# Another hand-written order for all 923 operations of a convolution and feed-forward kernel

## The chip, the cores and the metric

The kernel runs on one core of a Trainium2 chip. The core has a matrix engine (TensorE, PE in the profile), a vector engine (VectorE, DVE), a scalar engine (ScalarE, ACT), GpSimd (POOL), and SyncE (SP), whose work here is to issue DMAs. The engines run side by side; each takes its own instructions strictly in order, and waits on semaphores for what other engines and DMAs deliver. The metric is the time of one execution in microseconds (us), lower is better; a version's time is the median of its runs.

## The reference

One block of a network on a sequence of 2048 rows with 640 channels. A layer norm, a gated long convolution and a residual come first, then a second layer norm and a gated feed-forward layer (width 1728) with its own residual:

```python
def _A_ref(q, k, v, shift_k, ssm_k, ssm_D):          # q is layernorm(x)
    k_shift = sum over 4 taps t of k_pad[:, t:t+S, :] * shift_k[:, 3-t]
    kv = k_shift * v
    y = irfft(rfft(pad(kv)) * rfft(pad(ssm_k)))[:S]    # causal convolution over the sequence, per channel
    y = y + kv * ssm_D
    return q * y
def _B_ref(x, w_gate, w_up, w_down):
    return (silu(x @ w_gate) * (x @ w_up)) @ w_down
x  = A_q
h  = x + _A_ref(_layernorm(x), A_k, A_v, A_shift_k, A_ssm_k, A_ssm_D)
h2 = h + _B_ref(_layernorm(h), B_w_gate, B_w_up, B_w_down)
```

Inputs and output are bf16.

## The kernel before, in words

**Blocks.** The sequence is cut into four blocks (0 to 3) of 512 rows, each spread as 128 partitions by 4 rows (called r below). The convolution is done with transforms of length 1024 as matrix products: the filter block g (`load_g`, L289) is turned (`g_turned`) and transformed into a spectrum G; the block of k is turned and run through the four taps on PE (`kv_of`, L490), multiplied by v on DVE (L513 for block 0, L515 for the others), and transformed into a spectrum X (`transform`, PE L329, evicted from PSUM by ACT at L319 or by DVE at L322). `mac` (L524 to L594) adds up the products X[i]·H[j-i] on DVE, partly by accumulating DMAs which POOL issues (L243). `inverse` (L651) prepares sums and differences on DVE (L662 to L687), goes back through PE (L698), and ACT and DVE (L707, L709) apply the first layer norm, the gate and the residual. `turn_h` normalises the rows (L722 on ACT or L724 on DVE) and turns them, by DMA for blocks 1 and 2 (L404), by PE for blocks 0 and 3. `ffn` does gate and up products (PE L769), silu on ACT (L783), the product with `up` (either L785 on ACT followed by L787 on DVE, or L786 on DVE alone), and the down product (PE L845).

**Loads.** k comes by plain loads for block 0 and by transposing DMAs for the rest; g of blocks 1 to 3 is turned by ACT (L419) and transposing DMAs (L404); x, v and the weights come by plain loads (L301, L296, L737, L747).

**What sets the order.** The functions don't issue anything. Each calls `plan.add` and leaves an operation with a number, counted in the order of the calls. `Plan.run` then goes through the tuple `ORDER` (L47 to L89), which names every operation once, and issues them in that order. Since every engine has one queue, `ORDER` is the order of work on each engine and on SP's and POOL's DMA queues. Where an entry is negative, operation `~i` (one less than the number without the sign) goes to its other engine: a copy or product of ACT goes to DVE, a load of SP goes to POOL, an addition of DVE becomes an accumulating DMA of POOL. `ORDER` also decides which storage a tile gets: `Plan.run` hands out the 4 PSUM slots, the rows and the 22 units of the arena at the first use and takes them back after the last, so that another order makes other tiles share a unit, and with it other waits.

Operations spoken of below:

| number | what it is |
|---|---|
| 16, 17; 26; 27 | loads of k, v and x of block 0 |
| 12; 13, 14 | load of g of block 0; the two halves of the forward matrix WF |
| 186; 192; 191 | loads of g, x and v of block 1 |
| 194 to 197; 187 to 190 | the transposing DMAs of g and of k of block 1 |
| 97 | eviction of half a plane (128x320) of X of block 0 |
| 531 | normalised row (r = 1) of block 2 for the feed-forward part |
| 532, 534, 536, 538 | the four transposing DMAs of those rows of block 2 |
| 566 | the up product of one pair of chunks (128x1024) in block 1's feed-forward part; its L787 is 567 |
| 585, 803 | the up product of the odd chunk (128x512) in block 1's and block 2's feed-forward part; their L787 are 586 and 804 |
| 621 | load of v of block 3, which DVE's L515 reads |
| 714 | the first layer norm's power of block 3, on POOL |
| 715 to 720; 724 | DVE's preparation of the last inverse; its first product on PE |
| 829 | five chunks of a down product of block 2 |

A load's engine is chosen here:

```python
def load(nbytes, fn, w, r=()):
    return plan.add("sp", nbytes, lambda: fn(nc.sync), r, w, ("pq", nbytes, lambda: fn(nc.gpsimd)))
```

## Time and profile before

| | before |
|---|---|
| runs, us | 250.96, 251.34, 253.92; median 251.34 |
| span of the profiled execution, us | 251.4 |
| busy: PE, DVE, ACT, POOL | 94%, 79%, 69%, 21% |
| granted TensorE clock | 1.000 |
| DMA: bytes, share of the 16 engines | 33.66 MB; SP's queue 32.1%, POOL's 25.9% |

The profiled execution's own time is its span, 251.4 us, which is the median of the runs to 0.1 us; nothing lies around it that has to be added. The profile lists for each engine when it was busy and what ended each of its waits. PE's ends are modelled, because its matmuls are pipelined, so that a busy PE is not a PE at its peak; for PE the spacing of the starts in a run of equal matmuls is the better measure.

### The profile page before, as it was taken

What the parts mean: (1) busy time and instruction counts of PE and PEld (TensorE: products, weight loads), DVE (VectorE), ACT (ScalarE), POOL (GpSimd) and SP (SyncE); (2) the same over time, 40 slices, a digit from 0 to 9 for tenths busy, and PEclk for the clock granted to TensorE, in tenths of its full rate; (3) what the DMA queues carried; (4) which work ended last, traced back from release to release, by engine and by line L of the source; (5) the groups of instructions that cost most, each with busy time, mean ns of one, the idle gap of its engine ahead of it and who ended that gap; (6) DMA issues with size and microseconds to landing.
All of it is one profiled execution on the core that took longest, in us unless ns stands there. A gap on an engine that the chain in (4) does not pass through costs nothing.

```text
span 251.4 us, 5138 instructions
## 1 busy us (share of the span) xinstructions
PE 237.3 (94%) x2113; PEld 153.0 (61%) x2125; DVE 197.7 (79%) x249; ACT 173.9 (69%) x300; POOL 54.0 (21%) x54
## 2 busy tenths in 40 slices
PE   3869997999999999999999999999999999999994
PEld 3447675788777677444465676454456785465662
DVE  2379999999999999999999989999999542131222
ACT  2449998999999976975988789983542865325100
POOL 0002003231540313220270404263612110000030
PEclk9999999999999999999999999999999999999999
DMA  5995699774998654685345468889592200000052
GB/s 156 376 212 163 127 324 352 231 197 92 165 246 292 202 81 81 105 154 133 79 66 146 86 99 194 148 146 163 98 224 29 26 0 3 0 0 3 0 78 78
DMA packets 37283, 33.66 MB, mean 134 GB/s; under 512 B 22470, under 2 KB 32076, under 8 KB 37260
## 3 DMA queue, kind: packets, MB, share of 16 engines
q1 hardware_dynamic: 31884, 21.38, 32.1%
q0 software_dynamic: 5376, 11.96, 25.9%
q8 instruction: 16, 0.26, 0.4%
q14 instruction: 7, 0.06, 0.1%
HBM read 16.29 MB, written 4.59 MB: 83 GB/s over the span
## 4 chain that ended last, share of the span: by engine, by line
PE 56%; ACT 17%; DMA 10%; DVE 9%; issue 4%; SPq 3%; DVEq 0%; ACTq 0%; POOLq 0%
PE ps L769 24%; PE ps L845 22%; ACT arena L319 7%; DMA arena<-in_A_ssm_k_dram 7%; PE ps L698 5%; DMA arena<-arena 3%; ACT sg L785 2%; PE ps L490 2%; SPq L404 2%; ACT junk L606 1%; PE ps L329 1%; PE ps L833 1%; DVE arena L674 1%; DVE arena L663 1%; DVE arena L662 1%
## 5 line engine op out<-in xcount | busy, mean ns | idle before, releaser
L769 PE MATMUL ps<-arena,wgu 128*128 128x512 bf16 (+1 forms) x668 | 116.7, 328 | 1.4 <-ACT sg L809 0.5
L769 PEld LDWEIGHTS <-wgu 128*128 128x128 bf16 x680 | 66.2, 98 | 45.3 <-issue 1.4
L845 PE MATMUL ps<-wd,tT 128*128 128x320 bf16 x416 | 59.1, 299 | 0.0
L845 PEld LDWEIGHTS <-tT 128*128 128x128 bf16 x416 | 39.8, 98 | 17.2 <-issue 1.8
L542 DVE TENSOR_TENSOR arena<-arena 128x2560 bf16<-128x2560 bf16 x30 | 44.1, 1484 | 0.2
L783 ACT ACTIVATE sg<-ps 128x1024 bf16<-128x1024 f32 (+1 forms) x28 | 26.9, 968 | 20.3 <-PE ps L769 19.7
L329 PE MATMUL ps<-arena,WF 128*128 128x320 bf16 x176 | 29.8, 299 | 1.2 <-ACT arena L319 0.9
L785 ACT CAST sg<-ps 128x1024 bf16<-128x1024 f32 (+1 forms) x23 | 23.0, 998 | 6.9 <-PE ps L769 3.1
L319 ACT CAST arena<-ps 128x320 bf16<-128x320 f32 (+1 forms) x48 | 25.2, 583 | 1.9 <-DVE arena L545 1.1
L610 POOL TENSOR_TENSOR sm<-sm,neghalf 128x4 f32<-128x4 f32 (+1 forms) x10 | 16.6, 1659 | 43.4 <-DVE sm L646 43.1
L787 DVE TENSOR_TENSOR tT<-sg,sg 128x1024 bf16<-128x1024 bf16 (+1 forms) x23 | 15.5, 673 | 11.5 <-ACT sg L785 11.5
L243 POOL DMA_DIRECT2D arena<-arena x11 | 13.3, 1211 | 47.4 <-DVE arena L542 11.2
L329 PEld LDWEIGHTS <-WF 128*128 128x128 bf16 x176 | 17.1, 98 | 10.0 <-issue 2.3
L606 ACT ACTIVATE junk<-arena 128x640 bf16<-128x640 bf16 x28 | 20.8, 744 | 1.3 <-DVE arena L709 1.3
L545 DVE TENSOR_TENSOR arena<-arena 128x2560 bf16<-128x2560 bf16 x14 | 20.7, 1487 | 0.2
L319 ACT ACTIVATE arena<-ps 128x640 bf16<-128x640 f32 (+1 forms) x32 | 20.2, 655 | 0.3
L698 PE MATMUL ps<-arena,WI 128*128 128x320 bf16 x96 | 15.7, 299 | 0.9 <-issue 0.6
L850 ACT ACTIVATE row<-ps,sm 128x640 bf16<-128x640 f32 x12 | 9.5, 791 | 8.2 <-PE ps L845 8.0
L709 DVE SCALAR_TENSOR_TENSOR arena<-arena,sm,ps 128x640 bf16<-128x640 bf16 x16 | 13.6, 876 | 1.8 <-ACT ps L707 1.8
L852 POOL DMA_DIRECT2D out_dram<-row x12 | 11.7, 1153 | 14.1 <-ACT row L850 14.1
L707 ACT ACTIVATE ps<-ps,sm 128x640 f32<-128x640 f32 x16 | 12.1, 770 | 3.7 <-PE ps L698 3.5
L698 PEld LDWEIGHTS <-WI 128*128 128x128 bf16 x96 | 9.0, 97 | 5.6 <-issue 1.3
(91 smaller groups left out, 240.8 us busy)
## 6 DMA issues: line engine op xcount, KB each, us to landing
arena<-arena POOLq DMA_DIRECT2D x11, 640.0 KB, 6.1
arena<-in_A_q_dram SPq DMA_DIRECT2D x4, 640.0 KB, 5.1
out_dram<-row POOLq DMA_DIRECT2D x13, 160.0 KB, 4.2
arena<-in_A_ssm_k_dram SPq DMA_DIRECT2D x3, 640.0 KB, 9.4
arena<-in_A_v_dram SPq DMA_DIRECT2D x3, 640.0 KB, 6.3
wd<-in_B_w_down_dram SPq DMA_DIRECT2D x2, 800.0 KB, 7.3
out_dram<-arena POOLq DMA_DIRECT2D x2, 640.0 KB, 5.8
wgu<-in_B_w_gate_dram SPq DMA_DIRECT2D x1, 800.0 KB, 6.5
```

The lines of the kernel that those rows point to most:

```text
L319: (lambda: nc.scalar.activation(dst(), src(), ACT.Copy, scale=2.0)) if twice else (lambda: nc.scalar.copy(dst(), src())),
L329: nc.tensor.matmul(ap(ps)[:, h, 0:NH], w, ap(src)[:, r, h * NH:(h + 1) * NH], start=(first and i == 0), stop=(last and i == len(rs) - 1), ...
L542: dve(1402, lambda: v.tensor_mul(to(), X.part(xs), H.part(hs)), [X.at(xs), H.at(hs)], [at])
L545: added(1402 * n - 69 * (n - 1), lambda: v.tensor_add(to(), to(), b()), to, b, [what], at, n)
L606: act(725, lambda r=r: nc.scalar.activation(waste(), ap(x)[:, r, :], ACT.Square, scale=D ** -0.5, accum_out=sm(s, MSQ, (r,))), [(x, r)], [ ...
L610: nc.gpsimd.tensor_tensor(sm(s, RSTD, rs), sm(s, VAR, rs), ap(neghalf)[:, 0:len(rs)], op=ALU.pow)
L698: nc.tensor.matmul(ap(ps)[:, w, 0:NH], m, src[:, w * NH:(w + 1) * NH], start=(i == 0), stop=(i == len(terms) - 1))
L769: nc.tensor.matmul(split(ap(ps), n)[:, i, :], w(k), ap(hT)[:, k, lo:lo + n], start=(k == 0), stop=(k == KT - 1))
L783: act(905 if wide_ else 490, lambda: nc.scalar.activation(of(sg), of(*gate), ACT.Silu), [(gate[0], gate[1] + i) for i in range(m)] + (psu ...
L785: op = plan.add("act", 905 if wide_ else 490, lambda: nc.scalar.copy(of(co), of(*up)), psu + [sg], [co] + tt, ("dve", 1135 if wide_ else 6 ...
L787: op.rest = dve(602 if wide_ else 336, lambda: nc.vector.tensor_mul(to(), of(sg), of(co)), [sg, co], tt)
L845: nc.tensor.matmul(ap(ps[hf])[:, hf, 0:NH], ap(tT)[:, c * BLK + at:c * BLK + at + P], ap(wd)[:, c, hf * NH:(hf + 1) * NH], start=False, st ...
```

## The change

The code is the same but for the tuple `ORDER`: all 923 operations are still there, each once, and nothing is computed otherwise. The order of nearly all of them is another one on every engine and queue. The new tuple takes 42 lines in place of 43, so that every line behind it has a number one less. What else follows from it:

- **Engines.** Among SP's and POOL's DMAs, one goes elsewhere: 621, the load of block 3's v, is issued by SP, right behind the turns 532, 534, 538, 536 of block 2, and no longer by POOL. (The loads 616 of block 3's g, and the stores 308, 757 and 902 stay with POOL.) Of the copies and products, 97, 531, 566, 748 and 894 go from ACT to DVE in the new order, and 585, 803, 745 and 876 from DVE to ACT; of block 0's four k evictions two instead of three are DVE's (21, 23 for 19, 21, 25), of its four g evictions three as before (35 for 37).
- **Start.** SP's loads were k, shift taps, k, g1, v0, WF, skip, g0, WF, x0, WI, WI; they are k, taps, k, v0, g1, g0, WF, WF, skip, x0, one weight load of 640 KB, WI, WI.
- **Block 1.** SP's queue was: a turn of g1, x1's load (192), two turns of g1, then k1's turns with the last of g1's; it is: the eight turns (195, 194, 190, 196, 189, 197, 187, 188) and x1's load behind them. The turned g1 takes arena unit 4, which g0's raw tile held before it; in the old order it had unit 16.
- **Last inverse.** DVE's order was 715, 716, 717, 718, 719, 720; it is 715, 716, 718, 717, 720, 719. On PE, 829 stood ahead of 724 and stands behind it.
- **POOL's queue.** The stores 600, 615, 605, 610 of block 1 stand between the accumulating DMAs of block 3's `mac` instead of behind them, 757 stands ahead of them, and 714 behind them.

The diff, cut to the lines with those parts:

```diff
--- before.py
+++ after.py
 ORDER = (
-    0, 1, 2, 3, 16, 18, -20, 5, 4, 8, 17, 186, 9, 20, 22, 7, 10, 11, -22, 24, -26, 23, 26, 75, 76, 13, 15, 12, 6,
-    77, 78, 79, 193, 80, 81, 82, 34, 35, 14, 38, -40, 36, -38, 92, 32, 27, 93, 96, 97, 40, -42, 88, 89, 30, 94,
...
-    67, 68, 125, 115, 126, 116, 111, 112, 194, 198, 192, 199, 117, 69, 70, 195, 59, 60, 71, 72, 196, 200, 201, 63,
-    64, 61, 62, 73, 74, 127, 212, 65, 130, 66, 128, 202, 213, 207, 129, 134, 208, 131, 187, 203, 189, 197, 214,
-    215, 216, 190, 209, 210, 204, 133, 205, 270, 188, 221, 224, 225, 223, 175, 132, 138, 122, 211, 206, 217, 143,
...
-    631, 510, 514, 521, 522, 570, 573, 574, 644, 526, 622, -646, 595, 611, 617, 511, 515, 516, 512, 517, 518, 687,
-    525, 601, 612, 524, 527, 523, 528, 710, 682, 529, 530, 535, -534, 534, 531, 537, 532, 594, 596, 713, 646, 538,
...
-    598, 536, 806, 599, 805, 808, 650, 766, 765, 807, 809, 810, 811, 693, 709, 652, 654, 653, -622, 655, 695,
...
-    796, 798, 799, 812, 814, 815, 816, 705, 715, 716, 717, 718, 719, 600, 720, 605, 610, 817, 813, -758, 818, 819,
-    820, 821, 822, 823, 829, 724, 737, 723, 735, 738, 740, 736, 824, 830, 741, 739, 742, 743, 721, 725, 831, 832,
...
+    17, 8, 16, 1, 2, 0, 26, 186, 5, 3, 24, 7, 22, 4, -24, 9, 18, 10, 25, 11, 19, 20, -22, 75, 76, 77, 78, 79, 12,
+    80, 81, 82, 13, 83, 6, 40, -42, 38, 14, -40, 30, 193, 36, 37, 34, -36, 92, 93, 101, 102, 32, 96, -98, 94, 15,
+    95, 88, 89, 103, 104, 98, 84, 42, 85, 27, 120, 119, 118, 121, 90, 91, 99, 43, 44, 86, 87, 47, 48, 105, 106, 45,
+    46, 55, 56, 49, 174, 50, 51, 52, 107, 108, 29, 33, 57, 113, 58, 114, 53, 54, 100, 109, 124, 28, 110, 123, 126,
+    67, 68, 115, 116, 195, 111, 125, 194, 190, 112, 117, 69, 70, 198, 199, 31, 71, 72, 127, 196, 59, 60, 200, 201,
+    63, 189, 64, 73, 197, 61, 74, 130, 62, 212, 213, 187, 122, 65, 66, 128, 207, 208, 188, 202, 203, 192, 129, 214,
...
+    570, 521, 595, 611, 522, 644, 525, 573, 574, 526, 512, 517, 518, 511, 515, 706, 601, 602, 603, 612, -646, 516,
+    -758, 594, 606, 524, 527, 681, 523, 707, 528, 713, 682, 709, 687, 613, 596, 607, 529, 530, 614, 535, -532, 532,
+    537, -534, 534, 712, 604, 708, 538, 597, 598, 599, 647, 651, 649, 646, 608, 805, 536, 678, 648, 685, 677, 609,
+    650, 693, 680, 806, 810, 809, 765, 652, 807, 653, 600, 808, 811, 615, 766, 654, 769, 767, 621, 768, 770, 688,
...
+    799, 705, 821, 822, 812, 814, 815, 816, 715, 817, 716, 718, 717, 720, 719, 724, 714, 737, 829, 723, 735, 738,
+    740, 830, 736, 739, 741, 722, 818, 727, 742, 728, 831, 721, 725, 726, 824, 825, 730, 743, 729, 744, -752, 752,
...
```

61 rows, old and new, of the table ORDER are left out of this document.

## The prediction

> **What bounds the kernel now.** I read the page's busy times first, then the busy times by stretch, then the chain of waits, and last the order of time at the places that the change touches.
>
> ```profile
> span 251.4 us, 5138 instructions
> ...
> PE 237.3 (94%) x2113; PEld 153.0 (61%) x2125; DVE 197.7 (79%) x249; ACT 173.9 (69%) x300; POOL 54.0 (21%) x54
> ...
> DVE  2379999999999999999999989999999542131222
> ```
>
> PE is busy for 94% of the span and DVE for 79%, but DVE's row of slices (40 equal ones of 6.3 us) shows that its idle time lies at the ends: from the fifth slice to the thirty-first it is full. The stretches say it sharper; their columns are the stretch, its length, and the busy us (with instructions) of PE, PE's weight loads, DVE, ACT and POOL, then clock and DMA:
>
> ```profile
> 0.00:15.00 15.00, 7.93 (x174) 5.25 (x175) 5.80 (x16) 4.68 (x4) 0.54 (x6) 1.00 0.94 281
> 15.00:195.00 180.00, 176.59 (x1578) 113.73 (x1588) 174.90 (x200) 148.32 (x265) 49.37 (x43) 1.00 0.70 157
> 195.00:248.00 53.00, 52.79 (x365) 34.06 (x365) 16.46 (x34) 20.90 (x31) 4.04 (x6) 1.00 0.11 21
> 248.00:251.40 3.40, 0.00 (x0) 0.00 (x0) 0.53 (x1) 0.00 (x0) 0.00 (x0) 1.00 0.08 24
> ```
>
> Between 15 and 195 us both engines are full: PE is busy for 176.59 of 180 us and DVE for 174.90. So 3.4 us of PE and 5.1 us of DVE are all that any order can win back there. From 195 to 248 us only PE is full (52.79 of 53), and the last 3.4 us are the last result's way out.
>
> ```profile
> 194.60 1.09 PE ps L698 x8
> ...
> 240.78 7.18 PE ps L845 x52
> ...
> 247.98 0.55 DVE row L864
> ```
>
> The chain of waits (start, length, what) ends in PE work without a gap, and the last stretch of it, 52 matmuls in 7.18 us, gives PE's pace: 0.138 us per matmul of 320 columns. PE stops at 240.78 + 7.18 = 247.96. So the end is set like this: DVE works through to the last inverse, PE's first product of that inverse (L698, 194.44 below) is the meeting point, and behind it stands a fixed amount of PE work, 247.96 - 194.44 = 53.52 us, and then 251.4 - 247.96 = 3.44 us of tail. An order can gain by bringing the meeting point forward or by moving PE work ahead of it; it loses by the opposite.
>
> **The change part by part.** *Start.* PE's first large work waits for g of block 0.
>
> ```profile
> 3.09 0.43 SPq L903 DMA_DIRECT2D WF<-const_wf  x1
> ...
> 3.90 0.38 SPq L289 DMA_DIRECT2D arena<-in_A_ssm_k_dram  x1
> ...
> 11.13 3.15 DVE L513 TENSOR_TENSOR arena<-ps,arena 128x512 bf16<-128x512 f32 x6 [3.83 <-DMA arena<-in_A_v_dram]
> ...
> 14.96 1.03 PE L411 MATMUL ps<-ident,arena 128*128 128x128 bf16 x15 [2.98 <-DMA arena<-in_A_ssm_k_dram]
> ...
> 15.82 0.82 PE L329 MATMUL ps<-arena,WF 128*128 128x320 bf16 x4
> ```
>
> v0 was there at 11.13, g0 at 14.96 (the releasers say so), and between them landed half of WF and g0: 256 + 640 KB in 3.83 us, 4.3 ns per KB. The new queue has that half of WF behind g0, so g0 comes up to 256 x 4.3 = 1.1 us earlier. But the first product needs that half too, and before, it began 0.86 us after the first turn (15.82). All four turns of g0 now fill this time. I take a gain of 0.6; the bounds are 0 (everything still has to land) and 1.1. v0 now lands before g1; DVE's products with it (3.15 us) are then off the way, but DVE waits for g0 anyway: 0.
>
> *DVE's share.* The new order gives DVE work that ACT did, and the other way round.
>
> ```profile
> L787 DVE TENSOR_TENSOR tT<-sg,sg 128x1024 bf16<-128x1024 bf16 x22 | 15.1, 685 | 11.5 <-ACT sg L785 11.5
> ...
> L724 DVE TENSOR_SCALAR row<-arena,sm 128x640 bf16<-128x640 bf16 x6 | 2.5, 444 | 0.1
> ...
> L786 DVE TENSOR_TENSOR tT<-sg,ps 128x1024 bf16<-128x1024 bf16 x2 | 2.4, 1222 | 6.2 <-PE ps L769 6.2
> ...
> L786 DVE TENSOR_TENSOR tT<-sg,ps 128x512 bf16<-128x512 bf16 x3 | 2.0, 680 | 2.3 <-ACT sg L783 2.3
> ...
> L413 DVE COPY kT<-ps 128x640 bf16<-128x640 bf16 x3 | 1.4, 485 | 3.7 <-PE ps L411 3.7
> ...
> L864 DVE SCALAR_TENSOR_TENSOR row<-ps,sm,arena 128x320 bf16<-128x320 f32 x2 | 1.1, 550 | 2.1 <-PE ps L845 2.1
> ...
> L787 DVE TENSOR_TENSOR tT<-sg,sg 128x512 bf16<-128x512 bf16 x1 | 0.4, 417 | 0.0
> ```
>
> Ahead of the meeting point DVE gets 97, an eviction of 128x320, which no row shows on DVE: the copy from PSUM of twice the elements, but bf16, takes 0.485, the half row with two more operands 0.550; I take 0.45, with 0.35 and 0.55 as bounds. It gets 531, a normalised row: 0.444. It gets 566: 1.222 in place of 0.685, which is 0.537 more. It loses the direct products 585 and 803: twice 0.680 - 0.417 = 0.263, together 0.526. Sum: 0.45 + 0.444 + 0.537 - 0.526 = +0.90. ACT, busy for 148.32 of the same 180 us, takes what it gets into its idle time. The flips 745, 748, 876 and 894 lie behind 195 us, where DVE has room. Cost 0 there, and at most 0.5 each if DVE were full.
>
> *The last inverse.*
>
> ```profile
> 192.10 1.56 DVE L674 TENSOR_TENSOR arena<-arena 128x1280 bf16<-128x1280 bf16 x2
> ...
> 194.44 1.25 PE L698 MATMUL ps<-arena,WI 128*128 128x320 bf16 x8
> ```
>
> The two L674 are 717 and 718, and 724 on PE reads only what 718 writes. Before, 718 was the second and ended at 192.10 + 1.56 = 193.66; PE came at 194.44, having just done 829. Now 718 is first: half of 1.56, 0.78, earlier. And 829, ten matmuls of 0.138 = 1.38 us, stands behind 724: PE comes 1.38 earlier, and has 1.38 more to do afterwards.
>
> *Waits that DVE loses and gets.*
>
> ```profile
> 40.74 0.88 DVE L709 SCALAR_TENSOR_TENSOR arena<-arena,sm,ps 128x640 bf16<-128x640 bf16 x1
> ...
> 41.39 0.77 ACT L707 ACTIVATE ps<-ps,sm 128x640 f32<-128x640 f32 x1 [0.93 <-PE ps L698]
> ...
> 41.73 0.80 DVE L724 TENSOR_SCALAR row<-arena,sm 128x640 bf16<-128x640 bf16 x2
> ...
> 42.45 0.87 DVE L709 SCALAR_TENSOR_TENSOR arena<-arena,sm,ps 128x640 bf16<-128x640 bf16 x1
> ```
>
> ```profile
> 142.75 1.49 DVE L542 TENSOR_TENSOR arena<-arena 128x2560 bf16<-128x2560 bf16 x1
> 145.18 0.16 DVE L648 SCALAR_TENSOR_TENSOR sm<-sm 128x4 f32<-128x4 f32 x1 [0.94 <-POOL sm L610]
> ```
>
> At 145.18 DVE had idled 0.94 us for POOL's power; before it lay one product of 1.49 (682), in the new order two (682 and 687), which covers this wait: -0.94. At 40.74 it is the reverse: between the two L709 (154 and 152) lay the L724 pair (161, 164), which now come after. DVE then asks for ACT's second L707 at about 41.6, and ACT has it at 41.39 + 0.77 = 42.16: a new wait of 0.5, with 0 and 0.9 (the whole of 42.45 - 41.6) as bounds. Who waits behind it is all of DVE's queue.
>
> *v of block 3 by SP.* The issues there, and then the rows of such loads by queue (packets apart: times, KB, median us from issue to landing):
>
> ```profile
> 150.04 1.28 SPq L404 DMA_TRANSPOSE arena<-row  x1
> ...
> 151.73 0.62 POOL L296 DMA_DIRECT2D arena<-in_A_v_dram  x1 [6.59 <-DVE arena L542]
> ...
> 158.86 1.48 DVE L515 TENSOR_TENSOR arena<-arena 128x2560 bf16<-128x2560 bf16 x1
> ```
>
> ```profile
> arena<-in_A_q_dram SPq DMA_DIRECT2D x4, 640.0 KB, 5.1
> ...
> arena<-in_A_v_dram SPq DMA_DIRECT2D x3, 640.0 KB, 6.3
> ```
>
> POOL issued v at 151.73; SP does so behind four turns, of which the last started at 150.04 (1.28 long). The normalised rows come later by the second product ahead of them, less the idle time, 1.49 - 0.94 = 0.55, and one of them later by 0.45 on DVE, so that SP is free at about 152.3. The load takes 6.3 us by SP's median (row above), so it lands at 158.6. L515 wanted it at 158.86 and will want it at about 158.7. Cost 0, up to 1 if the load lands late; behind L515 everything on DVE waits. POOL is spared one issue of 0.62, which no one waited for.
>
> *POOL and the rest.* The stores moved ahead (757, 600, 615, 605, 610) each hold POOL for an issue and delay the accumulating DMAs by about that; DVE now takes those sums later in its own queue. 714 comes later, but has until ACT's last L707 behind 194.44. I cost both at 0; if that cover fails, it is an issue or two of 0.6 to 1.3 us.
>
> *Instruction packets.* One wait of PE in the middle of its work has no releaser.
>
> ```profile
> PE ps L698 <- issue: 0.6, 1, 0.6
> ```
>
> The columns are total us, times, longest: 0.6 us, once. The packets come by count of instructions, so that another order only puts other instructions at the same seams; I put 0 into the sum, and -0.6 as a bound. The Trainium skill (Runtime: NRT & Kernel Launch, Instruction fetch mechanics) says that an engine's instructions are streamed in blocks of 16 KiB while it runs and that crossing a block is mostly hidden. By that rule this term is 0 whatever the order does; by the row it is 0.6 at the most, so the row and the rule stand 0.6 us apart.
>
> **Sum.** 718 ends at 193.66 + 0.90 (share) - 0.60 (start) - 0.78 (place) - 0.94 + 0.50 (waits) = 192.74. PE comes at 194.44 - 1.38 - 0.60 = 192.46 and waits 0.3. From 192.74 on: 53.52 + 1.38 + 3.44 = 58.34. The span is 251.1, 0.3 less than the profiled 251.4; the median of the runs shown (251.34) is the profiled time to 0.1, so I forecast **251.1 us**, no change. With its bounds (start +0.6 or -0.5, wait -0.5 or +0.4, v up to +1, packets -0.6; PE's arrival as a floor unless PE too loses less) the forecast's own range is 250.2 to 252.7.
>
> **The rivals.**
>
> *Block 1's x comes late (slower).* Before, x1 was loaded at 13.28, between the turns; now its load stands behind all eight.
>
> ```profile
> 13.28 0.57 SPq L301 DMA_DIRECT2D arena<-in_A_q_dram  x1
> 13.90 4.44 SPq L404 DMA_TRANSPOSE arena<-arena  x2
> ...
> 26.17 2.53 SPq L404 DMA_TRANSPOSE kT<-in_A_k_dram  x2
> ...
> 32.08 0.82 ACT L606 ACTIVATE junk<-arena 128x640 bf16<-128x640 bf16 x1
> ```
>
> The turned g1 now takes the unit of g0's raw tile, so the first turn waits for PE's last turn of g0, about 15.8 (14.4 plus twenty turns at 1.03/15). A turn holds SP for 2.53/2 = 1.27 us when it goes well: 8 x 1.27 = 10.1, issue at 25.9, landing 5.1 later at 31.0. ACT's first reader, L606, stands at 32.08, now about 31.9. That fits by 0.9 us. But among the first ones two took 4.44 us: with four of eight at 2.22, SP gets to x1 at 29.8 and it lands at 34.9, 3.0 too late. ACT is full there and DVE waits for ACT's L707 just behind, so nearly all of it reaches the end: 254.1. It decides from a landing at 32 on. For it: SP's queue has no other room. Against: x1 has only 640 KB and most early traffic is over by then. Chance 0.19.
>
> *Both full engines lose less (faster).* If half of PE's 3.4 us between 15 and 195 goes and DVE keeps pace (half of its 5.1 is 2.5), and the start gives 1.1: 251.1 - 1.7 - 0.5 = 248.9; with all of PE's 3.4, 247.2. For it: these gaps are waits, and waits depend on the order. Against: other neighbours make other waits; the two that I could follow come to -0.94 and +0.50. Chance 0.24.
>
> *The change does nothing that can be seen.* The bytes, the instructions and the two full engines are the same; then 251.4, inside the forecast's own range. Chance 0.07. The forecast has the remaining 0.50.
>
> **Numbers.** The likeliest is 251.1. Against 251.34, 2% is 5.03 us: below 246.3 or above 256.4, which is about what a measurement of this kernel can tell from no change (its runs shown are 1.2% apart). The faster rival passes 246.3 only if all of PE's gaps go and the new wait (0.5) and the packet's (0.6) go too, 247.2 - 1.1 = 246.1: a sixth of its chance, 0.04. The slower passes 256.4 if x1 lands beyond 37 or v3's wait comes on top: half of its chance, 0.10. The rest, 0.86, is within. The range takes in the faster rival at its half-way price and the slower at its price, and leaves out a tenth on either side: 248.7 to 254.4.
>
> **What would show it.** Right: PE's first turn of g0 near 14.3 and its first L329 near 15.2; DVE busy for some 175 to 176 us in 15 to 195; the first late L698 starting right at the end of one L674, near 192.7, with PE waiting for it; no DVE wait for v before the third L515; PE without a gap behind. Wrong: ACT waiting for the DMA of A_q near 32 (the slower rival); PE busy for over 178 of 180 us in the middle (the faster one); a gap of PE behind 195, where I count none, since the rows of the last block would then come later than the order assumes.

## The result

| | before | changed |
|---|---|---|
| median of 20 runs each, us | 251.58 | 253.91 |
| lowest and highest | 250.43, 254.52 | 252.39, 255.16 |
| ratio, 95% interval | | 1.008 (1.006 to 1.010) |
| span of the profiled execution | 251.4 | 252.2 |

The changed kernel is slower by 0.8%. The forecast was 251.1, the range 248.7 to 254.4: the change is small, as forecast, and the time lies in the range, but it went up by 2.3 us where the sum had it 0.3 lower, and the forecast misses by 2.8 us. In the runs below, the ratios leave out the few executions that took over 1.5% longer than the fastest of their kernel.

1.7 us of these are a plain error. The changed kernel's profiled execution has a span of 252.2 and a time of 253.96, and in each of its runs the time lies 1.66 to 1.76 above the span. The prediction took the span of the shown trace for its time, with nothing around it to add. So the span that it worked out, 251.1, stood for a time of 252.8, and the shown trace of before, with a time of about 253.1, was one of before's late executions. What is left, 252.2 in place of 251.1, is 1.1 us in the sum. Against a usual execution of before (a second trace, below, has a span of 249.7) it is 2.5 us.

The page of the changed kernel, its busy times by stretch, and the chain of waits:

```profile
span 252.2 us, 5161 instructions
...
PE 239.0 (95%) x2125; PEld 153.2 (61%) x2125; DVE 197.8 (78%) x250; ACT 173.3 (69%) x300; POOL 58.7 (23%) x53
...
DVE  2669999999789999899999998999999642113413
```

```profile
0.00:15.00 15.00, 9.72 (x193) 6.72 (x194) 6.26 (x17) 5.65 (x7) 0.54 (x6) 1.00 0.85 290
15.00:195.00 180.00, 175.46 (x1564) 111.80 (x1562) 173.60 (x200) 146.95 (x264) 52.57 (x40) 1.00 0.72 155
195.00:248.00 53.00, 53.00 (x370) 34.36 (x368) 17.40 (x34) 20.68 (x31) 5.58 (x7) 1.00 0.13 21
```

```profile
46.70 0.08 DVE sm L645
...
46.85 7.56 POOL sm L609
...
62.81 7.49 DMA arena<-arena
...
70.39 1.50 DVE arena L581
...
241.61 7.18 PE ps L844 x52
```

Between 15 and 195 us PE is busy for 175.46 us where it was 176.59, and DVE for 173.60 where it was 174.90. Of the idle 3.4 and 5.1 us, which an order could win back there, nothing was won; 1.1 and 1.3 us were added to them. The chain of waits says where: it goes from DVE's request (L645) into one GpSimd instruction of 7.56 us, further on into an accumulating DMA of 7.49 us, and back to DVE. Neither this instruction nor this DMA was on the chain of the shown trace of before. From 77 us on PE waits nowhere for over 0.15 us, until 241.61 + 7.18, and the tail is as it was.

The next three fences are the request and the power of block 0's second layer norm (158 on DVE, 159 on POOL) in the shown trace of before; then, in the changed kernel, DVE's rows in order of time around the power; then the power itself and DVE's wait for the DMA:

```profile
48.44 0.16 DVE L646 SCALAR_TENSOR_TENSOR sm<-sm 128x2 f32<-128x2 f32 x1 [0.43 <-ACT junk L606]
...
48.68 1.88 POOL L610 TENSOR_TENSOR sm<-sm,neghalf 128x2 f32<-128x2 f32 x1 [7.30 <-DVE sm L646]
```

```profile
46.62 0.15 DVE L645 SCALAR_TENSOR_TENSOR sm<-sm 128x2 f32<-128x2 f32 x1
46.69 0.48 DVE L378 TENSOR_TENSOR arena<-arena 128x640 bf16<-128x640 bf16 x1
47.09 1.49 DVE L541 TENSOR_TENSOR arena<-arena 128x2560 bf16<-128x2560 bf16 x1
48.50 0.82 DVE L385 TENSOR_TENSOR arena<-arena 128x1280 bf16<-128x1280 bf16 x1
49.23 0.48 DVE L378 TENSOR_TENSOR arena<-arena 128x640 bf16<-128x640 bf16 x1
49.63 2.82 DVE L538 TENSOR_TENSOR arena<-arena 128x5120 bf16<-128x5120 bf16 x1
52.37 1.48 DVE L389 TENSOR_TENSOR arena<-arena 128x2560 bf16<-128x2560 bf16 x1
54.44 0.16 DVE L647 SCALAR_TENSOR_TENSOR sm<-sm 128x2 f32<-128x2 f32 x1 [0.59 <-POOL sm L609]
```

```profile
46.85 7.55 POOL L609 TENSOR_TENSOR sm<-sm,neghalf 128x2 f32<-128x2 f32 x1 [6.31 <-DVE sm L645]
...
70.39 1.49 DVE L581 TENSOR_TENSOR arena<-arena 128x2560 bf16<-128x2560 bf16 x1 [2.57 <-DMA arena<-arena]
```

The power begins at 46.85 and ends at 54.40. That is 0.55 us after the end (53.85) of DVE's product at 52.37, where DVE itself stops for the power (0.59 us). Before, the power took 1.88 us. Where no product of DVE runs beside it, an instruction of the same form takes 0.72:

```profile
199.46 0.72 POOL L609 TENSOR_TENSOR sm<-sm,neghalf 128x2 f32<-128x2 f32 x1 [3.31 <-DVE sm L645]
```

Behind the power on POOL's queue stand a store and the accumulating DMA 254 (55.14, lands at 62.22); 258 adds into the same tile and so comes behind that landing: it is issued at 62.81, lands at 70.30, and DVE waits for it for 2.57 us. (The profile names a product of DVE that ended at 62.81 as what 258 waited for. But with the pause earlier, below, 258 went out before that product had begun, and in the changed kernel's second trace, too, it went out 0.59 us behind the landing of 254.)

### The profile page after: what moved, and what is told of

Same layout as the page of the kernel before. It is cut to its first block, busy times and chain, and to the rows that moved or that the text cites. A ratio compares the mean times of both kernels' runs of the same rounds, so it can differ in the third digit from the quotient of the medians.

```text
span 252.2 us, 5161 instructions
## 1 busy us (share of the span) xinstructions
PE 239.0 (95%) x2125; PEld 153.2 (61%) x2125; DVE 197.8 (78%) x250; ACT 173.3 (69%) x300; POOL 58.7 (23%) x53
## 4 chain that ended last, share of the span: by engine, by line
PE 67%; DVE 13%; DMA 5%; POOL 3%; ACT 1%; issue 1%; SPq 0%; DVEq 0%
PE ps L768 36%; PE ps L844 23%; PE ps L328 4%; POOL sm L609 3%; DMA arena<-arena 3%; DVE arena L541 2%; DMA arena<-in_A_q_dram 2%; DVE arena L708 2%; PE ps L697 2%; PE ps L832 1%; PE ps L489 1%; DVE tT L786 1%; DVE arena L591 1%; DVE arena L392 1%; DVE arena L581 1%
## 5 line engine op out<-in xcount | busy, mean ns | idle before, releaser
L768 PE MATMUL ps<-arena,wgu 128*128 128x512 bf16 (+1 forms) x680 | 118.2, 329 | 2.2 <-ACT sg L784 1.6
L609 POOL TENSOR_TENSOR sm<-sm,neghalf 128x4 f32<-128x4 f32 (+1 forms) x10 | 20.1, 2013 | 42.9 <-DVE sm L645 42.6
L242 POOL DMA_DIRECT2D arena<-arena x11 | 15.0, 1359 | 47.5 <-ACT ps L706 19.1
L318 ACT ACTIVATE arena<-ps 128x640 bf16<-128x640 f32 (+1 forms) x31 | 19.5, 662 | 0.3 <-PE ps L328 0.3
L851 POOL DMA_DIRECT2D out_dram<-row x12 | 13.6, 1253 | 23.2 <-ACT row L849 23.2
L708 DVE SCALAR_TENSOR_TENSOR arena<-arena,sm,ps 128x640 bf16<-128x640 bf16 x16 | 13.6, 877 | 1.2 <-ACT ps L706 1.2
```

Source lines behind the costliest of these rows:

```text
L318: (lambda: nc.scalar.activation(dst(), src(), ACT.Copy, scale=2.0)) if twice else (lambda: nc.scalar.copy(dst(), src())),
L609: nc.gpsimd.tensor_tensor(sm(s, RSTD, rs), sm(s, VAR, rs), ap(neghalf)[:, 0:len(rs)], op=ALU.pow)
L708: dve(800, lambda r=r, ps=ps, s=s: v.scalar_tensor_tensor(two(ap(x)[:, r, :]), two(ap(x)[:, r, :]), sm(n1, MEAN, (r,)), half(ap(ps)), op0= ...
L768: nc.tensor.matmul(split(ap(ps), n)[:, i, :], w(k), ap(hT)[:, k, lo:lo + n], start=(k == 0), stop=(k == KT - 1))
```

## The experiments

Times are medians; the ratio is to the kernel before, run on the same chip, with its 95% interval. Where `ORDER` has the length of the changed one, line numbers are one less than those of before. In the diffs a number is an operation, in the order of `ORDER`.

### Second traces of both kernels

No edit.

> The kernel before, unchanged, as a second look. The shown trace of before has a span of 251.4 us, while the changed kernel's times lie 1.76 us above its spans. If the same offset holds here, the shown trace is a late one: theory A expects a span near 249.8 (251.58 - 1.76) and one wait less on VectorE or TensorE than in the shown trace. The rival, that the offset is only the changed kernel's, expects a span near 251.4 and the same waits.

> The changed kernel, unchanged, as a second look. Theory A: GpSimd's power of block 0's second layer norm (operation 159) is held up by VectorE's back-to-back products each time, about 7.5 us from start to end in place of 1.9, so that the second accumulating DMA (258) lands near 70 and VectorE waits for it for 1 us or more. Rival: that was an accident of the one profiled execution, and this trace shows 159 in 2 to 3 us and no wait of VectorE near 70 us; the time is then about 252.

Measured: before 252.09 beside 252.1, span of the profile 249.7; changed 254.45, ratio 1.010 (1.006 to 1.013), span 252.2. PE's rows of the start in before's second trace:

```profile
13.39 1.03 PE L411 MATMUL ps<-ident,arena 128*128 128x128 bf16 x15 [1.82 <-DMA arena<-in_A_ssm_k_dram]
14.25 0.82 PE L329 MATMUL ps<-arena,WF 128*128 128x320 bf16 x4
```

The offset holds (251.41 for a span of 249.7), and nearly all of the difference of 1.7 between the two traces of before lies in the start: g of block 0 landed at 13.34 and not at 14.91, and the first large product (L329) began at 14.25 and not at 15.82, 1.57 earlier. PE's wait with no releaser near 38 us (0.37 and 0.59) adds 0.22. DVE's wait of 0.94 at the power (145.18 in the shown trace) is in both. The changed kernel's second trace repeats the first: the power takes 7.55 us again, DVE waits 2.43 at 70.09. It is no accident.

### Give GpSimd its pause earlier

```diff
-    ..., 156, 158, 249, ..., 180, 244, 321, ..., 327, 159, 160, 251, ...
+    ..., 156, 158, 159, 249, ..., 180, 244, 160, 321, ..., 327, 251, ...
```

> The changed order with one VectorE operation moved: 160 (the second layer norm's last step, which waits for GpSimd's power) from behind 250 to right behind 244, five products earlier, as it stood in the order before. VectorE then pauses near 49.7 us until GpSimd has the power. Theory A (GpSimd can't work while VectorE's products run back to back): the power ends near 50.3 instead of 54.4, 254 is issued 4 us earlier, VectorE's wait of 2.57 us near 70 is gone, and the time falls by 1.5 to 2.5 us below the changed kernel's. Rival (the power takes long for another reason, or the wait is replaced by another): the power still takes over 5 us, or the time is the changed kernel's within 0.5.

(159 has another place in the tuple, but it is at the same place on POOL's queue, and it starts 0.24 us behind the start of its request, 0.23 in the changed kernel.)

Measured: 252.03, ratio 0.999 (0.996 to 1.002), so 1.9 to 2.4 below the changed kernel. POOL's, DVE's and PE's rows:

```profile
47.58 3.42 POOL L609 TENSOR_TENSOR sm<-sm,neghalf 128x2 f32<-128x2 f32 x1 [6.49 <-DVE sm L645]
...
51.73 1.29 POOL L242 DMA_DIRECT2D arena<-arena  x1
60.82 1.18 POOL L242 DMA_DIRECT2D arena<-arena  x1 [7.80 <-DVE arena L541]
```

```profile
51.03 0.16 DVE L647 SCALAR_TENSOR_TENSOR sm<-sm 128x2 f32<-128x2 f32 x1 [0.59 <-POOL sm L609]
...
69.91 1.49 DVE L581 TENSOR_TENSOR arena<-arena 128x2560 bf16<-128x2560 bf16 x1 [1.24 <-DMA arena<-arena]
```

```profile
74.68 1.25 PE L768 MATMUL ps<-arena,wgu 128*128 128x256 bf16 x10 [0.23 <-ACT sg L784]
```

The power ends 3.4 us earlier, when DVE stops at 160, and 254 is issued at 51.73. The time falls as theory A says. The wait near 70 is only halved, since 258 was issued at 60.82 and still landed at 69.82; but for PE this is enough: it waits 0.23 us at 74.68 where it waited 1.55 in the changed kernel (75.16). The profiled execution is one of the two longest of the twelve (253.43), with a late start. Counted from the first large product (15.75 here, 15.05 in the changed kernel) its span is 1.20 us shorter, about the 1.32 that PE no longer waits.

### Or take the DMA ahead of the power

```diff
-    ..., 327, 159, 160, ..., -309, ..., -255, ...
+    ..., 327, -309, -255, 159, 160, ...
```

> The changed order with GpSimd's store 308 and accumulating DMA 254 moved ahead of the power 159. Theory A: 254 is issued near 49 to 52 instead of 55.1, the second one (258) near 60, and lands by 67.8; VectorE's wait of 2.57 us near 70 is gone, its wait for the power stays (0.6 to 1.5 us near 54); the time falls by 1 to 2.5 us. Rival: GpSimd's issues are held up by VectorE as the power was, 254 is issued no earlier than 54, and the time stays within 0.5 of the changed kernel's.

Measured: 252.93, ratio 1.003 (1.000 to 1.006); 1.0 to 1.5 us below the changed kernel, the low end of theory A. 254 was issued at 48.10 and 258 at 59.09, and DVE still waited 2.79 us, until 70.00. So 258 lands near 70 whether it is issued at 59.1, 60.8 or 62.8. Here PE still waits 1.78 us at 74.77, and the profiled execution is the longest of the twelve (253.73), so where the gain of this move comes from isn't shown. In the DMA view of 57 to 71 us (issues, KB each, us to landing), the row of 258 in a usual execution of before, in the changed kernel, with the pause earlier and with the DMA first:

```profile
arena<-arena POOLq DMA_DIRECT2D x1, 640.0 KB, 6.1
```

```profile
arena<-arena POOLq DMA_DIRECT2D x1, 640.0 KB, 7.5
```

```profile
arena<-arena POOLq DMA_DIRECT2D x1, 640.0 KB, 9.0
```

```profile
arena<-arena POOLq DMA_DIRECT2D x1, 640.0 KB, 10.8
```

### Move what shares the DMA engines with it

SP's queue in the changed kernel in that stretch; the two issues of L745 are parts of the down weights, 800 and 480 KB (182 and 183), issued while 258 is on its way. Before, they went out from 70 us on.

```profile
64.68 2.85 SPq L745 DMA_DIRECT2D wd<-in_B_w_down_dram  x2
```

```diff
-    ..., 424, 182, 425, ..., 345, 183, 347, ..., 411, 410, 293, ...
+    ..., 424, 425, ..., 345, 347, ..., 411, 410, 182, 183, 293, ...
```

> The changed order with the loads 182 and 183 (800 and 480 KB of the down weights) moved on SyncE's queue from right behind the turns of block 2's g to behind the turn 410; nothing else. Theory B: the second accumulating DMA (258) lands near 70 in the three looks at the changed order whatever the time of its issue (59.1, 60.8, 62.8), because these loads share the DMA engines with it; with them later it lands about 6.1 to 6.6 us after its issue, near 69, VectorE's wait near 70 falls from 2.5 to about 1.5 us, and the time by about 1 us below the changed kernel's 254. Rival (theory A alone: only the power's delay counts): landing and time stay as they are within 0.4.

> Both moves: 160 right behind 244 (GpSimd gets its pause early) and the loads 182 and 183 behind the turn 410. Theory B with A: 258 is issued near 60.8 and lands near 67, VectorE's wait near 70 (2.57 us in the changed kernel, 1.24 with the first move alone) is gone or under 0.3, and the time lies 0.5 to 1.5 us below that of the first move alone (252.0), so below the kernel before by up to 1 us. Rival: the landing stays near 70 and the time at 252.

Measured: the loads alone 253.75, ratio 1.006 (1.003 to 1.008); with the earlier pause 251.86, ratio 1.000 (0.998 to 1.002). Alone, the landing came 7.1 us after the issue instead of 7.5, and the wait was 2.17 us: theory B is at most a small part here, since the DMA was issued late anyway. Together, it lands 5.9 us after its issue, and DVE no longer waits near 70 at all:

```profile
arena<-arena POOLq DMA_DIRECT2D x1, 640.0 KB, 5.9
```

With the power early, the loads made 3.1 us of the landing (9.0 and 5.9). Its first packet went 3.4 us after the issue with the loads near it, 4.5 with the DMA first, and 2.0 with the loads later. But the time doesn't show it: 1.000 beside 0.999 for the earlier pause alone, where theory B wanted 0.5 to 1.5 us. PE had only 0.23 us left to win there. So the power's delay is the cause of the loss. The loads explain the late landing, and no more.

### The two halves joined crosswise

```diff
-ORDER = (all of the changed order)
+ORDER = (the first 400 operations in the order of before, the rest in the changed order; and the reverse)
```

> The first 400 operations in the order of before (up to about 84 us, the start and the stretch of the two accumulating DMAs among them), all the rest in the changed order. Theory A and B: the loss lies in the first 400 operations, so this takes the time of the kernel before, 251.6 to 252.1, changed by the later parts alone: 0.8 gained at the last inverse, 0.94 at the wait of 145, about 1.7 lost in two new waits (near 106 and 158) and 0.9 of work moved to VectorE; together 251.5 to 252.5. Rival (the loss lies in the flips and the waits of the second half): 253 to 254.

> The reverse: the first 400 operations in the changed order, all the rest in the order of before. Theory A and B: VectorE still waits 2 to 3 us near 70, and the time stays near the changed kernel's, 253 to 254. Rival (second half): 251 to 252, less by the earlier start.

Measured: 253.29, ratio 1.005 (1.002 to 1.008), and 259.39, ratio 1.030 (1.028 to 1.033). The first lies in the range of the rival (253 to 254), the second above both. But the seam between the halves made waits that neither parent has: in the first DVE waits 1.28 us for another accumulating DMA at 103.99, and PE 1.44 with no releaser near 39 (0.59 and 0.37 in the traces of before); in the second PE waits 3.45 us for ACT at 106.10:

```profile
103.99 1.49 DVE L541 TENSOR_TENSOR arena<-arena 128x2560 bf16<-128x2560 bf16 x1 [1.28 <-DMA arena<-arena]
```

```profile
106.10 0.69 PE L329 MATMUL ps<-arena,WF 128*128 128x320 bf16 x2 [3.45 <-ACT arena L319]
```

So the joined halves decide nothing: the first time would suit the rival, but these waits of its own can account for it.

### The dummy products

PE's first rows of the changed kernel:

```profile
10.43 3.67 PE L881 MATMUL ps<-ident 128*128 128x512 bf16 x9 [1.00 <-DVE arena L512]
13.94 1.28 PE L410 MATMUL ps<-ident,arena 128*128 128x128 bf16 x20
15.05 2.12 PE L328 MATMUL ps<-arena,WF 128*128 128x320 bf16 x13
```

The nine dummy products (operation 6, L881) wait for a PSUM slot that DVE frees, begin at 10.43 and end at 14.10. g of block 0 had landed at 12.80.

```diff
-    ..., -22, 75, 76, ..., 13, 83, 6, 40, ...
+    ..., -22, 75, 6, 76, ..., 13, 83, 40, ...
```

> The changed order with one TensorE operation moved: the nine dummy products (operation 6) from behind 80 to right behind 75, where they stood before. In the changed kernel they wait until 10.4 us for a PSUM slot and then take 3.67 us in the profiled execution (2.10 in two others), so that they end at 14.1, after block 0's g has landed (12.8). Theory C: this eats the earlier landing; with them back, TensorE's first turn of g starts right at the landing (12.7 to 13.1 instead of 13.9), and the time falls by 0.5 to 1 us below the changed kernel's (254.0) with less spread. Rival: the first turn comes earlier, but the wait near 70 ends no earlier, and the time stays within 0.3.

> The three moves together: 160 behind 244, the loads 182 and 183 behind the turn 410, the dummy products 6 behind 75. Theories A, B and C: no wait of VectorE for the accumulating DMA near 70, first turn of g right at its landing; time 250.8 to 251.4, that is 0.5 to 1 us below the two moves (251.86) and below the kernel before by about 1 us (252.1 on these chips). Rival: the start is covered by a later wait, and it stays at 251.9.

Measured: alone 253.69, ratio 1.006 (1.004 to 1.009); with the other two moves 251.31, ratio 0.996 (0.994 to 0.999). Theory C holds only in part. Alone, the move can't be told from the changed kernel (1.008 and 1.010): PE's first turn began at 12.97, but most large products then waited for ACT's evictions of the turned g:

```profile
16.50 3.75 PE L328 MATMUL ps<-arena,WF 128*128 128x320 bf16 x26 [1.38 <-ACT arena L412]
```

With all three moves, the kernel is 0.4% faster than before and 1.0% faster than the changed kernel. Of the gain over two moves, 0.55 us, the runs tell little, since the intervals of the two ratios still touch, but the spread of the runs is 1.0 us (250.91 to 251.91) where it was 2.6.

### The engines that the change chose

```diff
-    ..., 767, 621, 768, ...
+    ..., 767, -622, 768, ...
```

> The changed order with block 3's v (621) issued by GpSimd again, at the same place of the order; nothing else. The prediction's step: no one waited for GpSimd's issue, v lands at 156 to 158 either way before VectorE's product near 158: the changed kernel's time within 0.3. Rival: the issue on GpSimd is held up by VectorE as the power was and holds up the accumulating DMA 679 behind it: 0.5 to 1.5 us slower.

Measured: 258.74, ratio 1.025 (1.021 to 1.029). Both expectations were too small. In this order two stores stand ahead on POOL's queue, so that v is issued at 155.23 instead of 152.23, DVE waits for it, and for ACT at three places behind it (0.61, 0.29 and 0.49 us, at 172.67, 190.03 and 192.62). PE waits 2.76 us at 164.37 for the product with v:

```profile
154.07 1.82 POOL L851 DMA_DIRECT2D out_dram<-row  x2 [7.99 <-ACT row L849]
155.23 1.21 POOL L295 DMA_DIRECT2D arena<-in_A_v_dram  x1
```

```profile
162.83 1.49 DVE L514 TENSOR_TENSOR arena<-arena 128x2560 bf16<-128x2560 bf16 x1 [2.72 <-DMA arena<-in_A_v_dram]
```

```diff
-    32, 96, -98, 94, ..., 457, -567, 567, ..., 535, -532, 532, ...
+    32, 96, 97, 94, ..., 457, 566, 567, ..., 535, 531, 532, ...
```

> The changed order with the three operations that VectorE got ahead of the meeting point given back to ACT (97, 531, 566 with its second product 567). The prediction's term: 0.45 + 0.444 + 0.537 = 1.43 us less of VectorE, and the 0.80 us that VectorE waits for TensorE at 566 goes too; VectorE works through to the last inverse, so the time falls by 1 to 2 us below the changed kernel's, if the wait near 70 doesn't take the part of 97 (0.49). Rival: ACT is as full there, its other work comes later and VectorE waits for that instead: the time stays within 0.5.

Measured: 258.09, ratio 1.023 (1.019 to 1.028), 4 us slower and not 1 to 2 faster. DVE, relieved of the 1.43 us of work that the prediction counted, waits 2.72 and 4.20 us for ACT instead:

```profile
106.91 0.69 DVE L786 TENSOR_TENSOR tT<-sg,sg 128x1024 bf16<-128x1024 bf16 x1 [2.72 <-ACT sg L784]
...
161.28 0.29 DVE L810 TENSOR_TENSOR tT<-sg,sg 128x256 bf16<-128x256 bf16 x1 [4.20 <-ACT sg L809]
```

ACT was busy for 148 of the 180 us in before, yet around 566 it has no room: between 97.7 and 107.5 us of this trace it stands still for 1.2 us in all. The prediction's sentence that ACT takes what it gets into its idle time was written for two other operations, and its mirror image, a price for DVE alone, is no price: in this order ACT has no room for them.

### What makes GpSimd miss its turn

```diff
-    ..., 156, 158, 249, 331, ...
+    ..., 156, 249, 158, 331, ...
```

> The changed order with one short VectorE product (249, 128x640) moved from behind 158 (the step that asks GpSimd for the power) to ahead of it, as before. In both looks at before GpSimd has the power 0.55 us after the end of 253; in the changed kernel the short product stands between, GpSimd misses the end of 253 too and is done only when VectorE stops, 7.55 us after its start. Theory A1 (the short product at the moment of the request makes GpSimd lose its turn): the power ends near 48.8, VectorE's wait at 160 is gone, 254 is issued near 49.6; the time falls to 251.5 to 252.3, as with 160 moved. Rival A2 (it is the place of 160 alone: GpSimd gets through only when VectorE stops): power and time as in the changed kernel, 253.7 to 254.4.

> The three moves and 249 ahead of 158. By A1 VectorE's 0.59 us wait at 160 goes too: 250.7 to 251.1, 0.2 to 0.6 below the three moves (251.31). By A2: 251.3, the same within 0.3.

and in the order of before, the reverse:

```diff
-    ..., 248, 249, 231, ..., 158, 159, 320, ...
+    ..., 248, 231, ..., 158, 159, 249, 320, ...
```

> The reverse of short_back: the order of before with the short product 249 moved behind 158 and its power 159. By A1 the power no longer ends 0.55 us behind 253 but only when VectorE stops at 160, at about 50.4 instead of 48.8, with a wait of VectorE of 0.6 us, and the accumulating DMA 254 is issued 1.6 us later; the time grows by 0.3 to 0.8 us. By A2 the power stays at 1.9 us and the time as it is within 0.2.

Measured: 254.42, ratio 1.006 (1.003 to 1.010); 251.61, ratio 0.996 (0.993 to 0.999); 252.12, ratio 0.999 (0.995 to 1.003). A1 has fallen: with 249 back, the power still takes 7.15 us; and in the order of before, with 249 behind the request, GpSimd has the power in 0.88 us:

```profile
48.09 7.15 POOL L609 TENSOR_TENSOR sm<-sm,neghalf 128x2 f32<-128x2 f32 x1 [6.71 <-DVE sm L645]
```

```profile
47.15 0.88 POOL L610 TENSOR_TENSOR sm<-sm,neghalf 128x2 f32<-128x2 f32 x1 [6.96 <-DVE sm L646]
```

A2 says too little as well: with the same neighbours on DVE (158, 253, 239, 244, 160) the power takes 1.88 us in before and ends behind the first product, and 3.02 in the kernel with four moves, where it ends only when DVE stops. So the neighbours in the order don't decide whether GpSimd gets the first seam, the place between two of DVE's instructions. What is shown: in all thirteen traces whose first half is the changed order or a variant of it, the power ends only when DVE stops; in six of seven traces whose first half is before's it ends earlier, and in the seventh (`before_tail_2`, below) at DVE's stop as well; and 160 close behind the request bounds the damage.

One sign separates all twenty traces. In the six with the early end, DVE had stood idle for 0.20 to 0.80 us, waiting for ACT, just ahead of its request 158 (0.43 in the row at 48.44 above). In the other fourteen, the seventh among them, DVE came to 158 without a gap. No run sets this gap on purpose, so that it is a sign and not yet a cause; and it is no rule for every power, since in the changed kernel that of the first layer norm (38.66) took 1.88 us and ended before DVE stopped, though DVE had no gap ahead of its request either.

### The terms of the second half, and of the start, alone

```diff
-    ..., 518, 687, 525, ..., 682, 529, ..., 716, 717, 718, 719, ..., 823, 829, 724, 737, ...
+    ..., 518, 525, ..., 682, 687, 529, ..., 716, 718, 717, 719, ..., 823, 724, 829, 737, ...
```

> The order of before with the two gains of the second half that the prediction counted, alone: 718 ahead of 717 with 829 behind 724, and 687 behind 682. By the prediction's terms: VectorE's wait of 0.94 us at the power goes, 718 comes another 0.78 earlier, TensorE comes 1.38 earlier and does 829 afterwards; the end moves by -0.94 - 0.78 + 0.60 = -1.1 us: 250.9 to 251.2 where before has 252.1. Rival (TensorE is the bound of the second half, so VectorE's gains end in its waiting): 251.8 to 252.3.

> The order of before with the two gains of the second half alone, once more for a trace. The first comparison gave 252.3 beside 252.3 (ratio 0.998, interval 0.994 to 1.002) where the prediction's terms, added up for VectorE alone, gave 1.1 us less. Theory D: TensorE has no idle time between 90 us and the meeting point, so that VectorE's gains only make VectorE early: the trace shows 718 done 1 to 1.7 us before TensorE's first product of the inverse (0.76 in before) and no wait of VectorE near 143, and the time is the kernel before's within 0.3. Rival (a new wait took the gains): a gap of TensorE of over 0.5 us that before doesn't have.

Measured: 252.29, ratio 0.998 (0.994 to 1.002), and 252.9, ratio 1.003 (0.999 to 1.006): the same as before, not 1.1 faster. The traces are of two long executions, the first with a granted TensorE clock of 0.66 and a time of 359.4, the second with a time of 255.35. The second shows a wait of DVE of 1.42 us for ACT at 144.17 in place of the 0.94, but whether an execution of the usual length has it, and so which of the two readings is right, isn't settled.

```diff
-    8, 17, 186, 9, ..., 23, 26, 75, 76, 13, 15, 12, 6, ..., 35, 14, 38, ...
+    8, 17, 26, 186, 9, ..., 23, 75, 76, 12, 13, 14, 15, 6, ..., 35, 38, ...
```

> The order of before with the changed order of the first loads alone: v of block 0 ahead of g of block 1, then g of block 0 ahead of both halves of WF. In five looks at kernels with the first loads of before, g of block 0 landed at 13.3 to 13.7 in three and at 14.8 to 14.9 in two; in all looks at the changed loads it landed at 12.2 to 13.2. Theory E (the load order helps by itself and the changed kernel lost it again to the dummy products and to ACT's order): TensorE's first turn of g near 12.9, its first large product (L329) near 14.0 to 14.4, the time 0.3 to 0.8 us below before, without runs near 254. Rival: WF, now later, holds the first large product at 14.5 or later, and the time stays within 0.2.

Measured: 251.53, ratio 0.998 (0.995 to 1.001), which isn't told from 1. g landed at 12.72 and the first large product began at 13.63, 0.62 earlier than in before's second trace. But the span of this trace is 249.7 as well. PE's waits with no releaser, here and in before's second trace:

```profile
37.54 2.08 PE L698 MATMUL ps<-arena,WI 128*128 128x320 bf16 x14 [0.98 <-issue]
```

```profile
37.49 2.08 PE L698 MATMUL ps<-arena,WI 128*128 128x320 bf16 x14 [0.37 <-issue]
```

Both go on at the same moment, 37.54 and 37.49, and the wait has grown by 0.61, as much as the start had gained (0.62). That PE waits there for its instructions is inferred, not shown: a packet of 16 KB on the instruction queue began at 35.23 in the trace of before and at 34.94 in this one, and in all six traces with this wait PE goes on 2.26 to 2.61 us behind the start of such a packet. Coming to this place earlier didn't bring the packet earlier by as much. Of the thirteen traces whose first half is the changed order or a variant, only the reverse join has the wait (0.31 at 38.14). The Trainium skill (Runtime: NRT & Kernel Launch, Instruction fetch mechanics) says that crossing a block is mostly hidden; here, if this is what PE waits for, it cost 0.26 to 1.44 us in five of the seven traces whose first half is before's.

## Why the prediction was right or wrong

**Span and time (wrong, 1.7 us).** The step "the median of the runs shown (251.34) is the profiled time to 0.1" compared a span with times. It also hid that the trace on which the sum rests was a late one, so that the start's gain was reckoned from a landing at 14.96, where before's second trace has 13.34 and two other traces of usual length with its first loads have 13.66 and 13.72.

**The start (right against the trace shown, not worth it against a usual run).** g landed at 12.80, and the first large product came at 15.05, 0.77 earlier than in the shown trace; 0.6 was forecast. Against before's second trace it came 0.80 later, since the dummy products now stand in its way. The step looked at when data lands and at whose turn it fills, and not at what PE has in its queue ahead.

**POOL and the rest (the step that failed).** "DVE now takes those sums later in its own queue ... I cost both at 0; if that cover fails, it is an issue or two of 0.6 to 1.3 us." This was said of the stores and sums of block 3, and there it held: behind 71 us DVE waits nowhere for a DMA in the changed kernel. What failed is that GpSimd's work in block 0 has no term in the sum and so stands at 0 without a reason: the power 159, and 254 and 258 behind it. The price there was 0.59 + 2.57 = 3.16 us of DVE. Of that, PE lost 1.55 (its wait for ACT at 75.16, where ACT in turn had waited 2.71 for DVE), and with the pause earlier this wait fell to 0.23 and the time to before's:

```profile
75.16 1.25 PE L768 MATMUL ps<-arena,wgu 128*128 128x256 bf16 x10 [1.55 <-ACT sg L784]
```

The prediction followed the waits on GpSimd as a matter of when it is asked and how long its instruction lasts (0.94 us at 145.18). That the duration itself can depend on DVE's work next to it could be suspected from the trace of before, where powers of one form (128x2) lasted 0.69, 0.72, 1.88 and 2.04 us. The Trainium skill (SBUF — State Buffer, section SBUF: two separate sides) has a rule for it: VectorE and GpSimd share a pair of ports, and of a VectorE instruction with two SBUF inputs and a GpSimd instruction that reads SBUF, whichever starts first holds it for the whole instruction and blocks the other. The times agree with it: most powers that ran beside DVE's products ended one of two times after the end of such a product, 0.55 to 0.57 or 0.87 to 0.91 us. They add what the rule doesn't say, that GpSimd can miss five seams in a row (46.85 to 52.37 above).

**The waits.** The 0.94 at 145.18 is gone, as forecast. The new wait near 42, priced at 0.5, isn't there: DVE's second L708 follows the first without a gap (40.70). Two that were not forecast came: 0.80 us at 105.91 and 0.92 at 157.91.

```profile
40.70 0.88 DVE L708 SCALAR_TENSOR_TENSOR arena<-arena,sm,ps 128x640 bf16<-128x640 bf16 x1
```

```profile
105.91 1.22 DVE L785 TENSOR_TENSOR tT<-sg,ps 128x1024 bf16<-128x1024 bf16 x1 [0.80 <-PE ps L768]
```

```profile
157.91 0.29 DVE L810 TENSOR_TENSOR tT<-sg,sg 128x256 bf16<-128x256 bf16 x1 [0.92 <-ACT sg L809]
```

**The last inverse and the sum (right behind the meeting point, wrong ahead of it).** 718 ended at 192.80 + 0.82 = 193.62, 0.9 later than forecast; PE's first product of the inverse came at 193.92, straight behind other PE work:

```profile
193.92 0.71 PE L697 MATMUL ps<-arena,WI 128*128 128x320 bf16 x4
```

From there to the end lie 252.2 - 193.92 = 58.3 us; 58.34 was forecast. What failed is "PE comes at 192.46 and waits 0.3": PE didn't wait for DVE, it came 1.46 later than that, about what it had lost at 75.16 (1.55). In before, too, PE was the later of the two at this point. So DVE's gains of 0.78 and 0.94 could at best keep DVE from being late, and the sum for DVE, though it agrees to 0.9 us, was the sum for the wrong engine. Counted for PE, between before's second trace (first large product 14.25, meeting point 192.70, end 249.7) and this one (15.05, 193.92, 252.2): 0.80 at the start, 178.87 - 178.45 = 0.42 up to the meeting point, and 58.28 - 57.00 = 1.28 behind it (829, 1.38), together the 2.5 us of the spans. 829's move should have brought PE 1.38 earlier to the meeting point; it came 0.42 later, so 1.80 was lost on the way, 1.55 of it at 75.16.

**v by SP (right in the time).** It landed at 156.79, and DVE didn't wait for it; 158.6 was forecast for the landing. That the move is needed in this order wasn't seen: the prediction says of POOL's issue that no one waited for it.

**The rivals.** x1 landed at 31.51 (31.0 was worked out, 32 the point from which it decides), and ACT waited 0.18 us for it: the load is on the chain, by a hair, and costs next to nothing. That both engines lose less didn't happen; they lost more. That the time lies in the range is luck: its upper end was set for a late x1 (254.1), and what took the time there was something else.

**DVE's share.** Its +0.90 can't be tested by itself, as the run with three operations given back shows.

## What to carry to other kernels

Compare a span with spans and a time with times, and look at two executions before one of them becomes the base of a sum. In a kernel where one engine never idles, do the sum for that engine, and count for the others only what makes it wait. A small GpSimd instruction that VectorE waits for later should have that waiting step close behind its request (0.9% here), and what is queued behind it on GpSimd should be able to bear the delay. Large loads issued around an accumulating DMA can push its landing back; here that alone cost no time that the runs show.

## What wasn't expected of the hardware

- One form of GpSimd instruction, a power on 128x2 elements, took 0.69 to 0.72 us where VectorE had no product beside it, and 7.55 or 7.56 us in each of seven traces beside back-to-back products of VectorE.
- An accumulating DMA of 640 KB landed 5.9 us after its issue, and 9.0 and 10.8 with 1,280 KB of plain loads issued around it.
- TensorE waited at about 37.5 us, for its instructions as it seems, and for longer when it came earlier (0.37, then 0.98, in two traces).
- Nine equal products of TensorE (128x512) took 2.10 us with the DMA first and 4.00 with the pause earlier, with the granted clock shown as 1.00 from 9 to 15 us in both. Why isn't shown.
